# A fused Mamba-2 scan and PReLU MLP on one Trainium2 core: the state products of a pair moved to stand between the outputs' products of the pair in front and their copies

## The chip, the cores and the metric

The kernel runs on one core of one Trainium2 chip. The core has a matrix engine (TensorE, PE in the profile; its weight loads are listed as PEld), a vector engine (VectorE, DVE), a scalar engine (ScalarE, ACT), a general engine (GpSimd, POOL) and a queue that issues transfers (SyncE, SP). Each engine works through its own list of instructions in order and waits on semaphores for the others. The metric is the time of one execution on the device in microseconds. Three runs of the kernel before gave 380.07 in the median, from 380.0 to 380.35.

## The reference

The first half is a chunked state-space scan (Mamba-2's SSD form) over 4 batches, 8 heads, 768 steps, head dimension 32 and state dimension 16; the second half is an MLP with PReLU over the resulting 3072 tokens of width 256, with d_ff = 2048. Cut to what is computed:

```python
# scan, per batch and head, chunk by chunk
L  = exp(cum_i - cum_j) * causal            # decays between steps of a chunk
M  = (C @ B.T) * L                          # Gram products times decays
y  = M @ x  +  (C @ state) * exp(cum)       # within the chunk + from the state before it
state = exp(sum(log a)) * state + sum_j decay_from_j * B_j (x) x_j
# MLP
h = y @ w_in                                # 256 -> 2048
g = max(h, 0) + alpha * min(h, 0)
out = g @ w_out                             # 2048 -> 256
```

All of it is in fp32.

## The kernel before

**The scan.** The kernel uses chunks of Q = 128 steps, 24 of them over the four batches (six per batch), and treats two at a time: pair 0 to pair 11 (`pair(gp)`, L416). A pair is a Python generator; every `yield` ends a stage, and `ssm(gp, stages)` (L905) lets it run on by that many stages. What a pair issues:

- the transposes of B and C (PE, L469) and their copy out of PSUM (ACT, L472, tile bc);
- the decays inside a chunk, by scans on DVE (L438, tile dec), eight per pair;
- C split over even and odd heads (ACT, L484, tile cz) and C times the decay from the chunk's start (POOL, L487, `c_decayed`, tile cd);
- B times the decay to the chunk's end (POOL, L385, `pair_loads`, tile bn);
- the **state products** bn x x (PE, L520, `added`), into a tile here called dps; the array is split in two by columns for them (128*64);
- the new states from them (DVE, L532; ACT, L529, for the first chunk of a batch) and their masked form sm (POOL, L535), both in `states`. The last pair of a batch (pairs 2, 5, 8, 11) needs one of its two blocks only;
- the Gram products C x B (PE, L570, `products_bc`), in four banks: two of the pool ps_s and, for pairs from 4 on, two of the pool ps_h (`spare()`), and their product with the decays (DVE, L606);
- the **outputs' products** (PE, L622 from the state and L629 within the chunks), into two tiles y, and their copies to SBUF (ACT, L636, tile xT).

**The MLP.** Four chunks make a group of 512 tokens (GC = 4, GT = 512); there are six groups. Group 0 is computed in the prologue by ordinary matmuls (`hidden`, `output`). Groups 1 to 5 take one level of a Strassen-like scheme with seven products in place of eight: `quad(g, z, after)` (L761) makes the four blocks of the hidden layer for a quarter z of d_ff (seven products `first`, L773, in two PSUM banks of ps_h, A and Y), applies PReLU (`prelu`, L751: ACT writes alpha times h, L756, and DVE takes the maximum, L758, column half by column half) to the blocks g12, g22, g21 and g11 in that order, and makes their differences on POOL (tc_, L807; ta, tb, td, L816). Its blocks go through seven products with w_out (`product`, L747) during the following quad. So the main loop (L1022) has 20 quads; z runs from 0 to 3 in each group.

**The order.** The schedule is written out by hand. `quad` calls `after(1)` to `after(14)` between its own steps, and `after(j)` issues what the tables hold for the place (z, j): `with_gram`/`without` the products of the quad before, `late_sums` the sums of weights for the scheme (POOL, L715; in the first three quads of the loop), `steps` one more stage of a pair, and the other places `combine` and `finish` (the end of the group before), `token_sums` (POOL, L727) and `pair_loads`. In group g the pairs 2g + 2 and 2g + 3 are worked on, for group g + 1 of the MLP. In the list below "(0, 9)" is the place z = 0, j = 9; a pair's two halves repeat with z + 2.

For pairs from 4 on (`fine`), the stages before the change stand at: transposes at (1, 12); the scans at (1, 14), (2, 1), (2, 2), (2, 5), with cz at the last; L520, L532, L535 and L487 at (2, 9); L570 and half of L606 at (2, 13); the rest of L606 at (3, 1); L622, L629 and L636 at (3, 5). bn is made at (1, 3) and (3, 8). The place j = 5 lies between DVE's L792 and the product of `first` that goes to the block c22 (DVE, L796); j = 9 between the PReLU of g21 and the product for g11; L802 is ACT's copy of m1 back to the bank Y, which that product adds to.

**Banks.** ps_s and ps_h have two banks each. Tiles from `ss_tile` take the banks of ps_s in turn: one for the transposes, one for dps, two for the Gram products, two for y, six per pair.

**Loads.** SP's list holds each pair's loads (`load_pair`, L139: ap, nat = B and C, xt = x, and abc, the decays spread over partitions); from pair 5 on they are issued at the start of the quads z = 0 and z = 2, more than a quad in front of the pair's transposes.

Of the kernel before, what the change touches and what calls it, by code (L numbers as in the profile page):

```python
# [9 lines left out]
F32 = mybir.dt.float32  # L10
U32 = mybir.dt.uint32
U16 = mybir.dt.uint16
ALU = mybir.AluOpType
# [9 lines left out]
def kernel(  # L23
# [25 lines left out]
    nc = tc.nc  # L49
# [6 lines left out]
    P = 128  # L56
    Q = 128
# [51 lines left out]
    def ss_tile():  # L109
        if early[0] is None:  # L110
            return ps_s.tile([P, 512], F32, name="ss")
        early[0] += 1
        i = early[0] % (3 if ident_p else 4)
        return ps_s.tile([P, 512], F32, name="ss") if i < 2 else bank(i)
# [211 lines left out]
    held = {}  # L326
    bns = {}

    def identity_bank():


        m5_bank.append(bank(3))
        nc.scalar.copy(out=m5_bank[0][:, HT:], in_=ident_h[:, :HT])
        ident_p.append(m5_bank[0][:, HT:])
# [42 lines left out]
    def pair_loads(gp):  # L377

        b, c = divmod(2 * gp, CPB)
        nat, abc, xt, ap = loads["p", gp]  # L380

        bn = work.tile([P, 2, H * N], F32, name="bn")
        i, bi = divmod(b, 2)
        pj = prt[i].rearrange("p (b h c) -> p b c h", b=2, h=H)[:, bi, c : c + 2]
        nc.gpsimd.tensor_tensor(  # L385
            out=bn.rearrange("p k (h n) -> p k h n", h=H),
            in0=nat[:, 0].rearrange("p k (h n) -> p k h n", h=H),
            in1=pj.unsqueeze(3).to_broadcast([P, 2, H, N]), op=ALU.mult)
        return bn
# [22 lines left out]
    def spare():  # L412

        return ps_h.tile([P, GT], F32, name="hp", tag="hp")

    def pair(gp):  # L416

        b, c = divmod(2 * gp, CPB)
        nat, abc, xt, ap = loads["p", gp]
        last = c + 2 == CPB  # L420
        dec = work.tile([P, 2, H, Q], F32, name="dec")
        dv = dec.rearrange("p k h t -> p k (h t)")

# [37 lines left out]
            yield  # L461


        tp = spare() if gp == 1 else ss_tile()
        if gp == 0:
            keep_warm(tp, 3, Q)
# [19 lines left out]
        def c_decayed():  # L486
            nc.gpsimd.tensor_tensor(out=cd.rearrange("p k t -> p (k t)"), in0=ct, in1=pf,  # L487
                                    op=ALU.mult)

        fine = gp >= 2 * GC // 2  # L490
        if gp < 2:
            spread_c()
        if gp == 0:
# [2 lines left out]
            dps = spare()  # L496
            keep_warm(dps, 6, Q)
            yield
        bn = bns.pop(gp) if gp in bns else pair_loads(gp)
        if gp == 1:  # L500
            c_decayed()
            dps = spare()
# [1 line left out]
        elif gp:  # L504
            yield

        nk = 1 if last else 2  # L510
        st = [masked.get(b)]
        new = work.tile([P, 2, P], F32, name="state")
        sm = work.tile([P, 2, P], F32, name="sm")

        def added(dps):
            dps = dps.rearrange("p (k m) -> p k m", m=P)
            for k in range(nk):
                for w in range(KC):
                    ws = slice(64 * w, 64 * w + 64)
                    nc.tensor.matmul(dps[ws, k], bn[:, k, ws], xt[:, k, w * P : (w + 1) * P],  # L520
                                     start=True, stop=True, tile_position=(0, 64 * w),
                                     skip_group_check=True)
            return dps

        def states(dps):
            for k in range(nk):
                old = state.get(b)
                if old is None:
                    nc.scalar.copy(out=new[:, k], in_=dps[:, k])  # L529
                else:  # L530
                    e = (k + 1) * Q - 1
                    nc.vector.scalar_tensor_tensor(out=new[:, k], in0=old, scalar=pf[:, e : e + 1],  # L532
                                                   in1=dps[:, k], op0=ALU.mult, op1=ALU.add)
                state[b] = new[:, k]
            nc.gpsimd.tensor_tensor(out=sm[:, :nk], in0=new[:, :nk],  # L535
                                    in1=hmask.unsqueeze(1).to_broadcast([P, nk, P]), op=ALU.mult)
            st.extend(sm[:, k] for k in range(nk))
            masked[b] = st[-1]

        if fine:  # L540
            for k in range(2):
                for w in range(2):
                    half_decays(k, w)
                    if k == 1 and w == 1:
                        spread_c()
                    yield
        else:
            if gp > 1:
                states(added(ss_tile()))
                c_decayed()  # L550
            decays(0)
            if gp == 1:
                dps = added(dps)
            if gp:
                yield
            if gp != 1:
                decays(1)
            if gp > 1:
                spread_c()
# [24 lines left out]
        if gp == 0:  # L584
            gram = products_bc()
            dps = added(dps)
            yield
            c_decayed()
            times(dec[:, :, :2], one_less(gram))
        elif gp == 1:  # L590
            gram = products_bc()
            g0 = one_less(gram)
            yield
            decays(1)
            states(dps)
            times(dec[:, :, :2], g0)
        else:
            if fine:
                states(added(ss_tile()))
                c_decayed()  # L600
            yield
            gram = products_bc()
        for i, r in enumerate(r for r in ((2, 3, 0, 1) if fine else (3, 2, 1, 0) if gp > 1 else range(4))
                              if r in gram):
# [6 lines left out]
        yield  # L611


        y = [ss_tile()[:, : 2 * Q].rearrange("p (k t) -> p k t", k=2) for w in range(KC)]
        if gp < 2:
            keep_warm(y[0].rearrange("p k t -> p (k t)"), 2 - gp)
        begun = False
# [7 lines left out]
        for k in range(2):  # L625
            for w in range(KC):
                for q in range(4):
                    h = 4 * w + q
                    nc.tensor.matmul(y[w][32 * q : 32 * q + 32, k], xt[:, k, h * D : (h + 1) * D],  # L629
                                     dec[:, k, h], start=False, stop=True,  # L630
                                     tile_position=(0, 32 * q), skip_group_check=True)
        g, q = divmod(2 * gp, GC)
        if q == 0:
            xts[g] = xtp.tile([P, KC, GT], F32, name="xT")
# [344 lines left out]
    for f in range(FIRST, NF):  # L979
        if f in (5, 10):  # L980
            load_pair(3 + f // 10)
        if f == 5:
            load_rows(1)
        hidden(0, f)
        if f <= 10:
            ssm(2)
        if f >= 9:
            ssm(3)
        for i in {FIRST: (5,), FIRST + 1: (6, 7)}.get(f, ()):
            convert_a(*pieces[i])  # L990
        convert_next(first=f > FIRST)
        if f == 8:
            bns[3] = pair_loads(3)
        if f == 8:
            rows_clamp(1)
            held["pr"] = rows_scan(1)
            rows_out(1)
        output(f - FIRST)
        if f in in_steps:
            weight_sums(wi, in_sums, 0, in_steps[f])  # L1000
    early[0] = None
    token_sums(1)
    ssm(2 * GC // 2, 2)


    steps = {(0, 1): 0, (0, 2): 0, (0, 5): 0, (0, 9): 0, (0, 13): 0, (1, 1): 0, (1, 5): 0,
             (1, 12): 1, (1, 14): 1, (2, 1): 1, (2, 2): 1, (2, 5): 1, (2, 9): 1, (2, 13): 1,
             (3, 1): 1, (3, 5): 1, (3, 12): 2, (3, 14): 2}

    late_sums = {(0, 2): ((wqt, out_sums, 0, 0),), (0, 4): ((wqt, out_sums, 0, 1),),  # L1010
# [11 lines left out]
    for i in range(NZ * (NG - 1)):  # L1022
        g, z = divmod(NZ + i, NZ)
        nxt = 2 * g + 2

        def after(j, g=g, z=z, i=i, nxt=nxt):
            places = with_gram if nxt < NP and z % 2 == 0 else without
            if i and j in places:
                product(*divmod(NZ + i - 1, NZ), places[j])
            if i == 0:  # L1030
                for f, half in last_out.get(j, ()):
                    output(NF - LATE + f, half)
            if (i, j) in ((0, 13), (1, 2)):
                store_first(i)
            for args in late_sums.get((i, j), ()):
                weight_sums(*args)
            if g > 1 and z == 0 and j in (5, 9, 13, 14):
                if j == 5:
                    comb[0] = combine(g - 1)
                next(comb[0], None)  # L1040
            if g > 1 and z in (1, 3) and j == 11:
                finish(g - 1, z // 2)
            if nxt + steps.get((z, j), NP) < NP:
                ssm(nxt + steps[z, j])
            if nxt < NP and (z, j) == (3, 7):
                token_sums(g + 1)
            ahead = nxt + {(1, 3): 1, (3, 8): 2}.get((z, j), NP)
            if ahead < NP:
                if ahead == 6:
                    rows_turn(1, held["pr"])  # L1050
                bns[ahead] = pair_loads(ahead)

        comb = [None] if i == 0 else comb
        if z == 0 and nxt < NP:
            load_pair(nxt + 1)
        if z == 2 and nxt + 2 < NP:
            load_pair(nxt + 2)
        quad(g, z, after)
# [31 lines left out]
```

## Time and profile before

| | |
|---|---|
| median of three runs | 380.07 us (380.0 to 380.35) |
| the profiled execution | 380.35 us, of it 378.6 span |
| PE busy | 368.0 us, 97% of the span |
| PEld busy | 294.0 us, 78% |
| DVE busy | 248.1 us, 66% |
| POOL busy | 201.3 us, 53% |
| ACT busy | 182.0 us, 48% |
| TensorE clock granted | 1.000 |
| L520, L629 one matmul instruction | 273 ns, x80 and x384 |
| L532 (DVE) | 340 ns, x16 |
| L535 (POOL), 128x256 | 0.73 us |
| L487 (POOL) | 0.73 us, x12 |
| L385 (POOL) | 0.64 us, x12 |

The profile is one execution on the chip. A line of the time line gives the start (us from the span's start), the time from first start to last end, the engine, the line of the program, the operation, the tiles written and read with their shapes, and the number of instructions merged in it; at its end stand the engine's idle time in front of it and what ended it. PE's matmuls overlap in the pipeline, so the distance from one start to the next tells more than a duration. An fp32 product of 128 rows and 256 columns appears as two matmul instructions.

### The profile page before, as it was taken

To read this page: it belongs to the slowest core of one execution; us is meant where nothing else is said; L and a number is where in the kernel's file an instruction comes from. 1 tells how busy PE (TensorE), PEld (TensorE's weight loads), DVE (VectorE), ACT (ScalarE), POOL (GpSimd) and SP (SyncE) were. 2 spreads that over 40 slices of the span, in tenths; PEclk is the share of its full clock that TensorE was granted. 3 is DMA by queue.
4 is the path that set the end of the run, shared out by engine and by line. 5 is a ranking of instruction groups with operands and counts; after the bars stand their busy time and mean duration, and the time that the engine had idled before them with its cause. 6 is when DMAs were issued, how large, how long until landed. Compare 5 with 4: busy or idle time off the path is not lost.

```text
span 378.6 us, 6134 instructions
## 1 busy us (share of the span) xinstructions
PE 368.0 (97%) x2223; PEld 294.0 (78%) x2223; DVE 248.1 (66%) x462; ACT 182.0 (48%) x384; POOL 201.3 (53%) x211
## 2 busy tenths in 40 slices
PE   8989999999999999999999999999999999999996
PEld 7666665677788788788788788788788788888884
DVE  7996979976448548738638748638747735554364
ACT  2647856435355245444445445435525525543541
POOL 4875666677919644724645535455354345355412
PEclk9999999999999999999999999999999999999999
DMA  7979998911176201004603702801801000101003
GB/s 136 196 156 331 253 281 187 179 29 56 59 123 116 65 3 55 2 0 69 140 3 55 153 2 47 164 0 35 173 4 22 9 0 11 19 0 30 1 0 83
DMA packets 121878, 30.71 MB, mean 81 GB/s; under 512 B 93736, under 2 KB 117752, under 8 KB 121848
## 3 DMA queue, kind: packets, MB, share of 16 engines
q1 hardware_dynamic: 116736, 29.74, 35.8%
q10 hardware_dynamic: 5112, 0.59, 1.1%
q8 instruction: 17, 0.28, 0.3%
q14 instruction: 13, 0.11, 0.1%
HBM read 26.98 MB, written 3.34 MB: 80 GB/s over the span
## 4 chain that ended last, share of the span: by engine, by line
PE 70%; DVE 15%; ACT 7%; DMA 3%; issue 2%; POOL 2%; SPq 0%; POOLq 0%; DVEq 0%; ACTq 0%
PE hp L773 28%; PE bank L747 26%; ACT gt L756 5%; DVE gt L758 5%; DVE dec L438 3%; PE bank L686 3%; PE ss L629 2%; PE hp L648 2%; PE hp L570 2%; DMA rows<-in_a_dram 2%; PE ss L622 1%; DVE wr L239 1%; DVE gt L652 1%; PE hp L663 1%; DVE state L532 1%
## 5 line engine op out<-in xcount | busy, mean ns | idle before, releaser
L758 DVE SCALAR_TENSOR_TENSOR gt<-hp,s_mul,gt 128x256 f32<-128x256 f32 x120 | 58.0, 483 | 51.3 <-ACT gt L756 50.2
L816 POOL TENSOR_TENSOR gt<-gt 128x512 f32<-128x512 f32 x58 | 73.8, 1272 | 33.0 <-PE bank L747 19.2
L756 ACT ACTIVATE gt<-hp,s_alpha 128x256 f32<-128x256 f32 x120 | 56.6, 474 | 66.8 <-DVE gt L758 36.4
L747 PE MATMUL bank<-gt,w_out 128*128 128x256 f32 x320 | 82.6, 382 | 0.0
L807 POOL TENSOR_TENSOR gt<-gt 128x512 f32<-128x512 f32 x20 | 25.4, 1272 | 81.1 <-DVE gt L758 70.7
L747 PEld LDWEIGHTS bank<-gt,w_out 128*128 128x128 f32 x320 | 60.1, 190 | 10.6 <-issue 2.3
L747 PE MATMUL bank<-gt,ws 128*128 128x256 f32 x240 | 58.3, 379 | 0.0
L747 PEld LDWEIGHTS bank<-gt,ws 128*128 128x128 f32 x240 | 45.1, 190 | 5.8
L438 DVE TENSOR_TENSOR_SCAN dec<-abc,bank 128x256 f32<-128x256 f32 x80 | 48.1, 661 | 0.0
L773 PE MATMUL hp<-xs,w_in 128*128 128x256 f32 x160 | 42.8, 390 | 0.0
L773 PE MATMUL hp<-xT,w_in 128*128 128x256 f32 x160 | 41.9, 384 | 0.0
L773 PE MATMUL hp<-xs,ws 128*128 128x256 f32 x160 | 41.1, 379 | 0.0
L792 DVE TENSOR_TENSOR hp<-hp,u 128x512 f32<-128x512 f32 x20 | 14.0, 700 | 37.5 <-ACT u L790 37.1
L773 PEld LDWEIGHTS hp<-xs,w_in 128*128 128x128 f32 x160 | 28.7, 189 | 7.7 <-issue 1.9
L773 PEld LDWEIGHTS hp<-xT,w_in 128*128 128x128 f32 x160 | 29.7, 190 | 5.2 <-ACT hp L802 1.0
L773 PEld LDWEIGHTS hp<-xs,ws 128*128 128x128 f32 x160 | 30.4, 190 | 4.1
L781 ACT COPY m<-hp 128x512 f32<-128x512 f32 x20 | 11.7, 586 | 41.0 <-PE hp L773 41.0
L686 PE MATMUL bank<-w_out,gt 128*128 128x256 f32 x128 | 31.0, 384 | 0.0
L686 PEld LDWEIGHTS bank<-w_out,gt 128*128 128x128 f32 x128 | 23.7, 190 | 6.6 <-issue 3.7
L796 DVE TENSOR_TENSOR c<-hp,m 128x512 f32<-128x512 f32 x20 | 13.6, 682 | 19.2 <-PE hp L773 19.2
L648 PE MATMUL hp<-xT,w_in 128*128 128x512 f32 x48 | 22.8, 598 | 0.5 <-DVE gt L652 0.3
L790 ACT COPY u<-hp 128x512 f32<-128x512 f32 x20 | 11.7, 586 | 22.5 <-PE hp L773 22.5
(156 smaller groups left out, 556.0 us busy)
## 6 DMA issues: line engine op xcount, KB each, us to landing
abc<-z SPq DMA_DIRECT2D x20, 512.0 KB, 5.3
raw<-in_moe_w_in_dram SPq DMA_DIRECT2D x8, 512.0 KB, 5.4
raw<-in_moe_w_out_dram SPq DMA_DIRECT2D x8, 512.0 KB, 6.5
xt<-in_x_dram SPq DMA_DIRECT2D x24, 128.0 KB, 2.9
out_dram<-o_sb SPq DMA_DIRECT2D x32, 64.0 KB, 1.9
nat<-in_B_dram SPq DMA_DIRECT2D x22, 64.0 KB, 3.4
nat<-in_C_dram SPq DMA_DIRECT2D x22, 64.0 KB, 2.8
ap<-pf SPq DMA_DIRECT2D x11, 128.0 KB
```

The lines of the kernel that those rows point to most:

```text
L438: nc.vector.tensor_tensor_scan(out=dv[:, k, hs], data0=abc[k][:, hs], data1=ident_p[0], initial=0.0, op0=ALU.mult, op1=ALU.add)
L648: nc.tensor.matmul(hp, w_in[:, k, f * P : (f + 1) * P], xts[g][:, k], start=(k == 0), stop=(k == KC - 1))
L686: nc.tensor.matmul(pos[0][t // 2][:, t % 2], gt[:, t * Q : (t + 1) * Q], w_out[:, f], start=(f == 0 and t % 2 == 0), stop=(f == NF - 1), s ...
L747: nc.tensor.matmul(ms[g][i][:, h], w, blocks[g, z][n][:, p], start=(q == 0 and h == 0), stop=(q == NQ - 1), skip_group_check=True)
L756: nc.scalar.mul(o[:, p], h[:, p], s_alpha[:, fs[p]])
L758: nc.vector.scalar_tensor_tensor(out=o[:, p], in0=h[:, p], scalar=s_mul[:, fs[p]], in1=o[:, p], op0=ALU.mult, op1=ALU.max)
L773: nc.tensor.matmul(to[:, p], w(2 * z + p), b, start=start and p == 0, stop=True, skip_group_check=True)
L781: nc.scalar.copy(out=m1, in_=A)
L792: nc.vector.tensor_tensor(out=Y, in0=Y, in1=u2, op=ALU.add)
L796: nc.vector.tensor_tensor(out=c22, in0=A, in1=m5, op=ALU.add)
L807: nc.gpsimd.tensor_tensor(out=tc_, in0=g22, in1=g12, op=ALU.subtract)
L816: eng.tensor_tensor(out=o, in0=x0, in1=x1, op=ALU.subtract)
```

## The change

The function `prelu` is left as it is. What the diff does:

- `added` and `states` (L520, L529, L532, L535) become the first two stages of a pair from 4 on, in front of its transposes; the block from the transposes to `c_decayed` is moved behind them unchanged.
- dps no longer takes a bank of its own: it lies in the second half of the bank of the second y of the pair in front (`beside`). Only pair 4, whose predecessor is not `fine`, takes a bank from `ss_tile`.
- A new `yield` stands between L629 and L636. At (1, 5) and (3, 5) four stages follow each other: the outputs' products of a pair, the state products of the next one, the copies L636 of the first, the states of the next.
- The steps at (0, 9) and (2, 9) go. `c_decayed` moves to the stage at (0, 5) and (2, 5), behind cz.
- `pair_loads` moves from (1, 3) and (3, 8) to (0, 9) and (2, 9); for pair 6 it takes `rows_turn` (L365: a transpose on PE, L368, and a copy on ACT, L372) with it. For pair 4 it is issued at f = 14 of the prologue, and that pair's first four stages run in front of the loop instead of its first two.

```diff
@@ -326,6 +326,8 @@
     held = {}
     bns = {}
+    beside = {}
+
     def identity_bank():
@@ -418,6 +420,7 @@
         b, c = divmod(2 * gp, CPB)
         nat, abc, xt, ap = loads["p", gp]
         last = c + 2 == CPB
+        fine = gp >= 2 * GC // 2
         dec = work.tile([P, 2, H, Q], F32, name="dec")
         dv = dec.rearrange("p k h t -> p k (h t)")
@@ -461,51 +464,6 @@
             yield
-        tp = spare() if gp == 1 else ss_tile()
-        if gp == 0:
-            keep_warm(tp, 3, Q)
-        for i in range(2):
-            for k in range(2):
-                nc.tensor.transpose(tp[:, (2 * i + k) * P : (2 * i + k + 1) * P], nat[:, i, k],
-                                    ident)
-        bc = work.tile([P, 4, Q], F32, name="bc")
-        nc.scalar.copy(out=bc.rearrange("p i t -> p (i t)"), in_=tp)
-        bh, ct = bc[:, :2], bc[:, 2:].rearrange("p k t -> p (k t)")
-        cz = czp.tile([P, 2, 2, Q], F32, name="cz")
-        cd = work.tile([P, 2, Q], F32, name="cd")
-
-        def spread_c():
-            for e in range(2):
-                o = cz[:, e].rearrange("p k t -> p (k t)")
-                if gp == 0 and e == 1:
-                    nc.gpsimd.tensor_scalar(out=o, in0=ct, scalar1=par[:, e : e + 1],
-                                            scalar2=None, op0=ALU.mult)
-                else:
-                    nc.scalar.mul(o, ct, par[:, e : e + 1])
-
-        def c_decayed():
-            nc.gpsimd.tensor_tensor(out=cd.rearrange("p k t -> p (k t)"), in0=ct, in1=pf,
-                                    op=ALU.mult)
-
-        fine = gp >= 2 * GC // 2
-        if gp < 2:
-            spread_c()
-        if gp == 0:
-            rows_turn(0, held.pop("pr"))
-            bns[0] = pair_loads(0)
-            dps = spare()
-            keep_warm(dps, 6, Q)
-            yield
-        bn = bns.pop(gp) if gp in bns else pair_loads(gp)
-        if gp == 1:
-            c_decayed()
-            dps = spare()
-            ahead[1] = spread(z, 1, lambda w: ss_tile())
-        elif gp:
-            yield
-
-
-
         nk = 1 if last else 2
         st = [masked.get(b)]
@@ -513,7 +471,7 @@
         sm = work.tile([P, 2, P], F32, name="sm")
         def added(dps):
-            dps = dps.rearrange("p (k m) -> p k m", m=P)
+            dps = dps[:, : 2 * Q].rearrange("p (k m) -> p k m", m=P)
             for k in range(nk):
                 for w in range(KC):
                     ws = slice(64 * w, 64 * w + 64)
@@ -538,11 +496,63 @@
             masked[b] = st[-1]
         if fine:
+            bn = bns.pop(gp) if gp in bns else pair_loads(gp)
+            dps = added(beside.pop(gp) if gp in beside else ss_tile()[:, : 2 * Q])
+            yield
+            states(dps)
+            yield
+
+
+        tp = spare() if gp == 1 else ss_tile()
...
+        if not fine:
+            bn = bns.pop(gp) if gp in bns else pair_loads(gp)
+        if gp == 1:
+            c_decayed()
+            dps = spare()
+            ahead[1] = spread(z, 1, lambda w: ss_tile())
+        elif gp:
+            yield
+
+        if fine:
             for k in range(2):
                 for w in range(2):
                     half_decays(k, w)
                     if k == 1 and w == 1:
                         spread_c()
+                        c_decayed()
                     yield
         else:
             if gp > 1:
@@ -595,10 +605,8 @@
             states(dps)
             times(dec[:, :, :2], g0)
         else:
-            if fine:
-                states(added(ss_tile()))
-                c_decayed()
-            yield
+            if not fine:
+                yield
             gram = products_bc()
         for i, r in enumerate(r for r in ((2, 3, 0, 1) if fine else (3, 2, 1, 0) if gp > 1 else range(4))
                               if r in gram):
@@ -611,7 +619,10 @@
         yield
-        y = [ss_tile()[:, : 2 * Q].rearrange("p (k t) -> p k t", k=2) for w in range(KC)]
+        ys = [ss_tile() for w in range(KC)]
+        y = [t[:, : 2 * Q].rearrange("p (k t) -> p k t", k=2) for t in ys]
+        if fine:
+            beside[gp + 1] = ys[1][:, 2 * Q :]
         if gp < 2:
             keep_warm(y[0].rearrange("p k t -> p (k t)"), 2 - gp)
         begun = False
@@ -629,6 +640,8 @@
                     nc.tensor.matmul(y[w][32 * q : 32 * q + 32, k], xt[:, k, h * D : (h + 1) * D],
                                      dec[:, k, h], start=False, stop=True,
                                      tile_position=(0, 32 * q), skip_group_check=True)
+        if fine:
+            yield
         g, q = divmod(2 * gp, GC)
         if q == 0:
             xts[g] = xtp.tile([P, KC, GT], F32, name="xT")
@@ -989,6 +1002,8 @@
         for i in {FIRST: (5,), FIRST + 1: (6, 7)}.get(f, ()):
             convert_a(*pieces[i])
         convert_next(first=f > FIRST)
+        if f == 14:
+            bns[4] = pair_loads(4)
         if f == 8:
             bns[3] = pair_loads(3)
         if f == 8:
@@ -1000,11 +1015,11 @@
             weight_sums(wi, in_sums, 0, in_steps[f])
     early[0] = None
     token_sums(1)
-    ssm(2 * GC // 2, 2)
-
-
-    steps = {(0, 1): 0, (0, 2): 0, (0, 5): 0, (0, 9): 0, (0, 13): 0, (1, 1): 0, (1, 5): 0,
-             (1, 12): 1, (1, 14): 1, (2, 1): 1, (2, 2): 1, (2, 5): 1, (2, 9): 1, (2, 13): 1,
+    ssm(2 * GC // 2, 4)
+
+
+    steps = {(0, 1): 0, (0, 2): 0, (0, 5): 0, (0, 13): 0, (1, 1): 0, (1, 5): 0,
+             (1, 12): 1, (1, 14): 1, (2, 1): 1, (2, 2): 1, (2, 5): 1, (2, 13): 1,
              (3, 1): 1, (3, 5): 1, (3, 12): 2, (3, 14): 2}
     late_sums = {(0, 2): ((wqt, out_sums, 0, 0),), (0, 4): ((wqt, out_sums, 0, 1),),
@@ -1042,9 +1057,14 @@
                 finish(g - 1, z // 2)
             if nxt + steps.get((z, j), NP) < NP:
                 ssm(nxt + steps[z, j])
+
+                if j == 5 and z % 2:
+                    for p in (1, 0, 1):
+                        if nxt + z // 2 + p < NP:
+                            ssm(nxt + z // 2 + p)
             if nxt < NP and (z, j) == (3, 7):
                 token_sums(g + 1)
-            ahead = nxt + {(1, 3): 1, (3, 8): 2}.get((z, j), NP)
+            ahead = nxt + {(0, 9): 1, (2, 9): 2}.get((z, j), NP)
             if ahead < NP:
                 if ahead == 6:
                     rows_turn(1, held["pr"])
```

More of the change, by code (lines that the diff above doesn't have):

```diff
@@ L461, in pair, with added, states @@
             yield
+        nk = 1 if last else 2
+        st = [masked.get(b)]
+        new = work.tile([P, 2, P], F32, name="state")
+        sm = work.tile([P, 2, P], F32, name="sm")
+        def added(dps):
+            dps = dps[:, : 2 * Q].rearrange("p (k m) -> p k m", m=P)
+            for k in range(nk):
+                for w in range(KC):
+                    ws = slice(64 * w, 64 * w + 64)
+                    nc.tensor.matmul(dps[ws, k], bn[:, k, ws], xt[:, k, w * P : (w + 1) * P],
+                                     start=True, stop=True, tile_position=(0, 64 * w),
+                                     skip_group_check=True)
+            return dps
+        def states(dps):
+            for k in range(nk):
+                old = state.get(b)
+                if old is None:
+                    nc.scalar.copy(out=new[:, k], in_=dps[:, k])
+                else:
+                    e = (k + 1) * Q - 1
+                    nc.vector.scalar_tensor_tensor(out=new[:, k], in0=old, scalar=pf[:, e : e + 1],
+                                                   in1=dps[:, k], op0=ALU.mult, op1=ALU.add)
+                state[b] = new[:, k]
+            nc.gpsimd.tensor_tensor(out=sm[:, :nk], in0=new[:, :nk],
+                                    in1=hmask.unsqueeze(1).to_broadcast([P, nk, P]), op=ALU.mult)
+            st.extend(sm[:, k] for k in range(nk))
+            masked[b] = st[-1]
+        if fine:
[4 more added lines that the diff above has]
+            yield
         tp = spare() if gp == 1 else ss_tile()
@@ L505, in pair @@
             yield
[L510 to L515, printed above, removed]
-            dps = dps.rearrange("p (k m) -> p k m", m=P)
[L517 to L529, printed above, removed]
-                else:
[L531 to L538, printed above, removed]
         if fine:
```

## The prediction

> **What bounds the kernel now.** I read the page's chain first, then the time line of the main loop, where the change sits, then the waits of the lines that it touches.
>
> ```profile
> PE 70%; DVE 15%; ACT 7%; DMA 3%; issue 2%; POOL 2%; SPq 0%; POOLq 0%; DVEq 0%; ACTq 0%
> ```
>
> PE carries the chain for most of the span, DVE and ACT for 22%. The time line says where. In the odd quads of a group (z = 1 and 3), which hold the outputs' products of a pair (L622, L629), PE issues without a gap:
>
> ```profile
> 163.06 1.08 PE L629 MATMUL ss<-dec,xt 128*32 128x128 f32 x32
> 163.99 0.65 ACT L636 COPY xT<-ss 128x256 f32<-128x256 f32 x2 [1.52 <-PE ss L629]
> 164.07 1.13 PE L773 MATMUL hp<-xs,w_in 128*128 128x256 f32 x4
> 165.03 1.03 PE L773 MATMUL hp<-xT,ws 128*128 128x256 f32 x4
> 165.24 0.69 DVE L796 TENSOR_TENSOR c<-hp,m 128x512 f32<-128x512 f32 x1 [2.04 <-PE hp L773]
> ```
>
> The reader is to see that ACT (1.52 us idle) and DVE (2.04) have room here and PE none: what is added to PE is paid. In the even quads (z = 0 and 2), which hold the state products L520 and the Gram products L570, it is otherwise (pair 7):
>
> ```profile
> 180.95 0.58 ACT L802 COPY hp<-m 128x512 f32<-128x512 f32 x1
> 181.19 0.66 PE L520 MATMUL ss<-xt,bn 128*64 128x128 f32 x8
> ...
> 181.77 1.13 PE L773 MATMUL hp<-xT,w_in 128*128 128x256 f32 x4
> ...
> 182.48 0.99 ACT L756 ACTIVATE gt<-hp,s_alpha 128x256 f32<-128x256 f32 x2 [0.55 <-DVE gt L758]
> ...
> 183.39 0.72 DVE L532 SCALAR_TENSOR_TENSOR state<-state,ap,ss 128x128 f32<-128x128 f32 x2
> ...
> 184.03 0.48 DVE L758 SCALAR_TENSOR_TENSOR gt<-hp,s_mul,gt 128x256 f32<-128x256 f32 x1
> ...
> 185.05 0.48 DVE L758 SCALAR_TENSOR_TENSOR gt<-hp,s_mul,gt 128x256 f32<-128x256 f32 x1 [0.54 <-ACT gt L756]
> 185.59 0.48 PE L570 MATMUL hp<-cz,bc 32*128 32x256 f32 x1 [0.32 <-DVE gt L758]
> ```
>
> The Gram products need both hp banks, so their second half starts only when the PReLU of g11 has left the second one. In all eight quads it starts 1.56 us after g11's first L758 (184.03 to 185.59 here; 94.52 to 96.08, 125.02 to 126.58, 154.64 to 156.20, 213.39 to 214.95, 242.62 to 244.18, 272.13 to 273.69, 301.37 to 302.93): ACT and DVE taking turns on one bank are the gate. PE, whose first half takes 0.65, is there 0.0 to 0.9 us earlier. So L520 here is mostly cover-filling: without it PE would wait for L802 (ends 181.53, next product 181.77) and again at the gate.
>
> **The change, part by part.** prelu itself is not edited. What moves is, for pairs 4 to 11, L520, L532 and L535 out of the even quad into the odd quad before it (pair 4's in front of the loop), the products c·decay (POOL L487) from (z even, 9) to (z even, 5), bn (POOL L385) to (z even, 9), and prt's transpose and copy (L368, L372) from (3, 8) to (2, 9).
>
> *New place on PE (cost).* From L520's first issue to the next product is 0.59 us for two blocks (x8: 181.19 to 181.77, 151.96 to 152.55) and 0.37 for one (x4: 122.21 to 122.58, the last pair of a batch). With the slower first issue on each side (0.86 became 0.96) the detour is 0.79 and 0.57. In the new place L629 already pays for leaving and re-entering the full array, so I take 0.59 and 0.37. Bounds: 0.43 and 0.22 if nothing but the streams counts (eight of 0.108, two at a time), 0.79 and 0.57 if the whole detour is paid again. Four pairs of two blocks (6, 7, 9, 10) and three of one (5, 8, 11): 4 x 0.59 + 3 x 0.37 = 3.5 us (2.4 to 4.9). Pair 4's products come at 81.73, between back-to-back L686 and L469: 0.75. Together 4.2 us (3.1 to 5.7).
>
> *Old place (gain).* Only the gate counts. What ends last for g11's first L758 once L532 and L529 are gone: pair 4, L715 on DVE, which moves up with it, 0.64 earlier; pair 5, g21's L758, 0.24 earlier, less most of prt's copy (0.22), now in ACT's queue there: 0.1; pair 6, ACT's mul behind L835, 0.18; pair 7, g21's L758, 0.53; pair 8, ACT's mul behind L835, 0.02; pair 9, 0.25 (L529 goes from ACT too); pair 10, 0.41; pair 11, 0.26. Sum 2.4 us. PE arrives earlier by L802's slack and the saved exit, 0.1 to 0.3, which just keeps it in front of the gate.
>
> *POOL.* Its queue is in order, and one row shows what happens when DVE wants SBUF operands while POOL works:
>
> ```profile
> 121.47 1.28 POOL L715 TENSOR_TENSOR w_out<-w_out 128x512 f32<-128x512 f32 x1
> ...
> 121.66 1.36 DVE L758 SCALAR_TENSOR_TENSOR gt<-c,s_mul,gt 128x256 f32<-128x256 f32 x1
> ```
>
> The instruction takes 0.47 elsewhere; here it ended 0.27 after POOL's. The c·decay product (0.73) now stands between the L715s of the first and third quad and pushes the last one into this L758. The third quad loses 0.3 to 0.7 at the gate (0.4 taken; it gains 0.4 if both L758 slip between two L715s); in the first the 0.4 that DVE waits for ACT covers it. In later quads c·decay, bn and prt's work meet idle POOL time (5.10 in front of L807 at pair 7), at no cost. If nat came late, bn would hold L816 behind it; for pair 8 nat's last part is issued at 178.37 and lands about 3.4 later, bn is due near 183.
>
> The Trainium skill, "Trainium Architecture — The Big Picture", section "What this means for kernel authors", says that VectorE and GpSimd share one port pair under an exclusive lock. The row agrees with it. By that rule also the L727s, which sm (L535) now pushes towards g22 in z = 3, would each cost a wait; DVE's 0.40 idle before g21 covers it.
>
> *New waits in the odd quad.* dps shares a bank with y[1]. ACT and DVE wait for each other on the two halves of one bank already (36.4 us of L756 waiting for L758), so I expect the second copy L636 to wait for L520 and L532 for that copy. Queued behind: on ACT the mul of g12 (1.51 us of room), on DVE c22, L796 (2.04 of room; L532 ends about 1.7 after L629, c22's operand comes at 1.8), on POOL sm and then, in z = 3, four L727 whose result is first read a quad later. Nothing on the path. SP's queue keeps its order: loads are not moved.
>
> *Sum.* 4.2 - 2.4 + 0.4 - 0.1 (L368's gap in z = 3) = +2.1 us. The profiled execution took 380.35 (span 378.6 and 1.75 around it), 0.3 over the median of 380.07; on the median that is 382.2. Ends: 3.1 - 2.8 = +0.3 and 5.7 - 1.4 = +4.3.
>
> The skill speaks for the change: "TensorEngine Tiling (Array Packing)", "Key Properties", says that changing the tiling mode drains the array. Put next to L629, L520 costs one mode change fewer per pair, and by that rule alone the sum would be about -1.6 us (an estimate: eight times the 0.2 by which 0.79 exceeds 0.59). The trace agrees on the price (0.10 in front, 0.16 and 0.10 behind L520), but the place left is one where PE waits anyway.
>
> **Rivals.**
> *A: as summed,* 382.2, from 381.0 to 383.5.
> *B: nearly free.* L520 overlaps L629's tail (both split the columns) and the third quad's L758 slip through: +0.3 to +0.6, 380.5. For it: eight matmuls stream only 0.43. Against: L570 to L520, from split array to split array, still shows a gap at 11.40.
> *C: faster.* The even quads give back the whole detour, because the gate follows PE rather than the turns of ACT and DVE: 5 x 0.79 + 3 x 0.57 = 5.7 against 3.1 to 4.2 paid, -1.5 to -2.6, about 378. It decides from 0.53 us of gate per quad on (4.2 over 8); the chain view gives 0.30. Against: g11's first product is done at about 182.3, before ACT is free for it at 182.95, in pair 7. For it: pairs 8, 9 and 11 have PE within 0.2 of the gate, so both limits are close and another order of events could move them together.
> *D: slower still.* The one-bank order makes c22 late in the odd quads, or POOL's queue holds L816: from 0.1 us after c22's due time on it reaches the PReLU chain. At 0.2 to 0.4 in seven quads, 383.6 to 385.
>
> **How the numbers follow.** Chances: A 0.55, B 0.13, C 0.17, D 0.15. About 0.2% (0.76 us) can be told from no change here. Faster is C and a trace of B, 0.18; same is the rest of B and A's lowest end, 0.14; slower A and D, 0.68. The range 380.2 to 384.0 leaves out C and D's upper part, some 2 in 10.
>
> **What would show it.** Right: L520 directly behind L629, the next L773 about 1.6 us after L629's first issue instead of 1.0; in even quads L773 waiting for ACT L802 and L570 for DVE L758, with odd quads 0.4 to 0.6 longer and even ones 0.0 to 0.6 shorter. L758 (from c) at 0.9 or more in the third quad. Wrong: even quads shorter by 0.6 or more throughout (C), L520 taking under 0.45 beside L629 (B), L796 waiting for L532 (D).

## The result, and the profile after

The changed kernel took 382.24 us (median of four runs, 381.66 to 383.0) against 380.03 (379.58 to 380.35): ratio 1.006, 95% interval 1.0037 to 1.0083. It is slower, by 2.2 us; the profiled execution took 381.83, its span 379.9 against 378.6. The mechanism of the forecast held: the state products are paid in full in the odd quads, and the even quads give back less.

The chain of the page, after:

```profile
PE 79%; DVE 8%; ACT 7%; SPq 2%; DMA 2%; issue 1%; ACTq 0%; POOL 0%; POOLq 0%
```

PE's share is 79% where it was 70%, and DVE's 8% where it was 15%, but most of this is not the change. In the stretch ahead of the first quad the chain held 29 us of PE and 27 of DVE before, and 57 and 4 after; the page of `e8_decay_late` below, which is the changed kernel but for one POOL instruction per pair, shows 70% and 12% again. From the first quad on, PE's part went from 234 to 241 us and DVE's from 31 to 25. The waits say more. PE's, after, from the list of who waited for whom (us in total, times, longest):

```profile
PE hp L786 <- ACT hp L815: 2.6, 8, 0.4
...
PE hp L580 <- DVE gt L771: 1.1, 2, 0.6
```

and before:

```profile
PE hp L570 <- DVE gt L758: 2.2, 5, 0.9
```

Eight times PE now waits for ACT's copy of m1 to Y (L802 before, L815 after) where it used to run the state products, a wait that the list of before does not have. The wait at the gate, the start of the second half of the Gram products (L570 before, L580 after), has fallen from 2.2 us in five places to 1.1 in two.

The odd quad that was shown of before, in the time line after (L640 is the former L629, L478 the former L520, L649 L636, L490 L532, L786 L773, L809 L796):

```profile
163.42 1.08 PE L640 MATMUL ss<-dec,xt 128*32 128x128 f32 x32
164.35 0.37 ACT L649 COPY xT<-ss 128x256 f32<-128x256 f32 x1 [1.52 <-PE ss L640]
164.43 0.66 PE L478 MATMUL ss<-xt,bn 128*64 128x128 f32 x8
165.02 1.13 PE L786 MATMUL hp<-xs,w_in 128*128 128x256 f32 x4
165.13 0.37 ACT L649 COPY xT<-ss 128x256 f32<-128x256 f32 x1 [0.41 <-PE ss L478]
165.54 0.73 DVE L490 SCALAR_TENSOR_TENSOR state<-state,ap,ss 128x128 f32<-128x128 f32 x2 [1.98 <-ACT xT L649]
165.98 1.03 PE L786 MATMUL hp<-xT,ws 128*128 128x256 f32 x4
166.19 0.69 DVE L809 TENSOR_TENSOR c<-hp,m 128x512 f32<-128x512 f32 x1
```

From L640's first issue to the next product of the MLP it is 1.60 us (163.42 to 165.02), before 1.01 (163.06 to 164.07): the state products cost 0.59 beside the outputs' products. The second copy waits for them and the state updates wait for that copy, but L809 starts 1.17 us after the first issue of the product that it reads (165.02 to 166.19), as before (164.07 to 165.24): those waits are off the path.

The even quad of pair 7, after (L771 is the former L758, L769 L756, L580 L570); the first line is the quad's first product:

```profile
173.33 1.03 PE L786 MATMUL hp<-xT,w_in 128*128 128x256 f32 x4
...
181.18 1.03 PE L786 MATMUL hp<-xs,w_in 128*128 128x256 f32 x4
...
182.54 1.13 PE L786 MATMUL hp<-xT,w_in 128*128 128x256 f32 x4 [0.33 <-ACT hp L815]
...
183.43 0.84 ACT L769 ACTIVATE gt<-hp,s_alpha 128x256 f32<-128x256 f32 x2 [0.55 <-DVE gt L771]
...
183.94 0.88 DVE L771 SCALAR_TENSOR_TENSOR gt<-hp,s_mul,gt 128x256 f32<-128x256 f32 x2 [0.54 <-ACT gt L769]
...
185.36 0.48 DVE L771 SCALAR_TENSOR_TENSOR gt<-hp,s_mul,gt 128x256 f32<-128x256 f32 x1 [0.54 <-ACT gt L769]
...
185.90 0.48 PE L580 MATMUL ss<-cz,bc 32*128 32x256 f32 x2
```

Two lines of the same quad before, beside those of the prediction:

```profile
172.38 1.03 PE L773 MATMUL hp<-xT,w_in 128*128 128x256 f32 x4
...
180.23 1.03 PE L773 MATMUL hp<-xs,w_in 128*128 128x256 f32 x4
```

The place of the state products is empty and PE idles there: from one product's first issue to the next it is 1.36 us (181.18 to 182.54), before with the state products between them 1.54 (180.23 to 181.77). The gate did move: the quad starts at 173.33, so the second half of the Gram products starts 12.57 us into it (185.90); before 13.21 (185.59 less 172.38).

**Where the time went.** The next table gives each quad's length, from the first issue of its first product (`first` into A from b11) to that of the next quad, read from the time lines of PE.

| quad (pair whose state products were in it, or now are) | before | after | difference | forecast |
|---|---|---|---|---|
| 1st, z = 0 (4 left) | 16.80 | 16.15 | -0.65 | -0.64 |
| 2nd (5 added) | 14.37 | 14.75 | +0.38 | +0.37 |
| 3rd, z = 2 (5 left) | 15.26 | 15.36 | +0.10 | +0.3 |
| 4th (6 added) | 14.49 | 14.97 | +0.48 | +0.5 |
| 5th (6 left) | 15.13 | 14.96 | -0.17 | -0.18 |
| 6th (7 added) | 14.16 | 14.74 | +0.58 | +0.59 |
| 7th (7 left) | 15.23 | 14.59 | -0.64 | -0.53 |
| 8th (8 added) | 14.38 | 14.75 | +0.37 | +0.37 |
| 9th (8 left) | 14.98 | 14.96 | -0.02 | -0.02 |
| 10th (9 added) | 14.38 | 14.96 | +0.58 | +0.59 |
| 11th (9 left) | 14.85 | 14.59 | -0.26 | -0.25 |
| 12th (10 added) | 14.15 | 14.75 | +0.60 | +0.59 |
| 13th (10 left) | 15.37 | 14.96 | -0.41 | -0.41 |
| 14th (11 added) | 14.38 | 14.75 | +0.37 | +0.37 |
| 15th (11 left) | 14.85 | 14.59 | -0.26 | -0.26 |
| 16th to 19th | 50.50 | 50.50 | 0.0 | 0 |

The odd quads gained 3.36 us, the even ones lost 2.31; the loop is 1.05 longer. In front of it stand pair 4's state products: from the last L686 of the prologue to the first quad it was 2.16 us (80.01 to 82.17) and is 2.90 (79.50 to 82.40), +0.74. Together +1.79; the rest of the difference of the medians (2.2) lies within what the prologue varies by (at the end).

### The profile page after: what moved, and what is told of

It is laid out like the page before. It is cut to its first block, busy times and chain, and to the rows that moved or that the text cites. A ratio compares the mean times of both kernels' runs of the same rounds, so it can differ in the third digit from the quotient of the medians.

```text
span 379.9 us, 6122 instructions
## 1 busy us (share of the span) xinstructions
PE 369.1 (97%) x2223; PEld 295.2 (78%) x2223; DVE 250.0 (66%) x462; ACT 182.2 (48%) x384; POOL 201.0 (53%) x211
## 4 chain that ended last, share of the span: by engine, by line
PE 79%; DVE 8%; ACT 7%; SPq 2%; DMA 2%; issue 1%; ACTq 0%; POOL 0%; POOLq 0%
PE hp L786 28%; PE bank L760 26%; PE bank L699 7%; PE hp L661 6%; ACT gt L769 5%; DVE gt L771 4%; PE ss L640 2%; PE hp L580 2%; PE ss L633 1%; PE ss L478 1%; DMA nat<-in_B_dram 1%; PE ss L511 1%; PE hp L676 1%; DVE dec L441 1%; SPq L163 1%
## 5 line engine op out<-in xcount | busy, mean ns | idle before, releaser
L771 DVE SCALAR_TENSOR_TENSOR gt<-hp,s_mul,gt 128x256 f32<-128x256 f32 x120 | 57.7, 483 | 50.7 <-ACT gt L769 49.5
L769 ACT ACTIVATE gt<-hp,s_alpha 128x256 f32<-128x256 f32 x120 | 56.3, 472 | 65.2 <-DVE gt L771 34.7
L786 PE MATMUL hp<-xT,w_in 128*128 128x256 f32 x160 | 41.9, 384 | 2.6 <-ACT hp L815 2.6
L786 PE MATMUL hp<-xs,w_in 128*128 128x256 f32 x160 | 42.8, 390 | 0.0
L786 PE MATMUL hp<-xs,ws 128*128 128x256 f32 x160 | 41.1, 379 | 0.0
L786 PEld LDWEIGHTS hp<-xT,w_in 128*128 128x128 f32 x160 | 29.7, 190 | 9.4 <-ACT hp L815 5.8
L786 PEld LDWEIGHTS hp<-xs,w_in 128*128 128x128 f32 x160 | 28.8, 189 | 7.5 <-ACT u L803 1.3
L786 PEld LDWEIGHTS hp<-xs,ws 128*128 128x128 f32 x160 | 30.4, 190 | 4.1
L493 POOL TENSOR_TENSOR sm<-state,bmask 128x256 f32<-128x256 f32 (+1 forms) x12 | 7.9, 661 | 34.3 <-DVE state L490 34.1
L803 ACT COPY u<-hp 128x512 f32<-128x512 f32 x20 | 11.7, 585 | 22.5 <-PE hp L786 22.5
```

Source lines behind the costliest of these rows:

```text
L769: nc.scalar.mul(o[:, p], h[:, p], s_alpha[:, fs[p]])
L771: nc.vector.scalar_tensor_tensor(out=o[:, p], in0=h[:, p], scalar=s_mul[:, fs[p]], in1=o[:, p], op0=ALU.mult, op1=ALU.max)
L786: nc.tensor.matmul(to[:, p], w(2 * z + p), b, start=start and p == 0, stop=True, skip_group_check=True)
L803: nc.scalar.copy(out=u2, in_=A)
```

## The experiments

Each run is compared with runs of the kernel before taken beside it, whose median was 379.62 us for the first four and 379.51 for the last three.

**The price of the new place.** `e3_twice` is the kernel before with the products issued a second time:

```diff
-        y = [ss_tile()[:, : 2 * Q].rearrange("p (k t) -> p k t", k=2) for w in range(KC)]
+        ys = [ss_tile() for w in range(KC)]
+        y = [t[:, : 2 * Q].rearrange("p (k t) -> p k t", k=2) for t in ys]
...
+        if fine:
+            added(ys[1][:, 2 * Q :])
         g, q = divmod(2 * gp, GC)
```

> The kernel before with the state products of pairs 4 to 11 issued a second time, between the outputs' products and their copies, into the second half of the second bank of y; nobody reads them. It is the price of the new place by itself, nothing is taken from the old one. Theory: five pairs of two blocks at 0.59 us and three of one at 0.37, all on PE in the odd quads: +4.1 us, 384.1. Rival B (the products overlap the tail of the outputs' products): five at 0.43 and three at 0.22, +2.8 us, 382.8. If odd quads had room on PE: 380.0.

Measured 383.52 against 379.62: ratio 1.0101, 1.0086 to 1.0116, +3.9 us. Odd quads +0.60, +0.37, +0.58, +0.58, +0.37, +0.59, +0.58, +0.37 (pairs 4 to 11), +4.04 in all; every even quad within 0.03 of before. Time line, the odd quad with pair 6's outputs:

```profile
163.03 1.08 PE L630 MATMUL ss<-dec,xt 128*32 128x128 f32 x32
164.04 0.66 PE L520 MATMUL ss<-xt,bn 128*64 128x128 f32 x8
164.63 1.13 PE L776 MATMUL hp<-xs,w_in 128*128 128x256 f32 x4
```

The products start when the outputs' products have run their 1.01 us and take 0.59 themselves. Rival B, an overlap with the tail, falls, and so does any room on PE in odd quads.

**What the old place cost.** `e2_no_products` leaves the state products of pairs 4 to 11 out:

```diff
             if fine:
-                states(added(ss_tile()))
+                ss_tile()
+                states(bmask.rearrange("p (k m) -> p k m", m=P))
                 c_decayed()
```

> The kernel before without the state products of pairs 4 to 11 (left out: the states take a constant tile in SBUF in their place, so the outputs that follow from the states are others); everything else stays in its place. Theory (gate): PE only waits longer in the even quads, for ACT's copy of m1 and for the gate, which DVE sets; 0.0 to 0.3 us gained in all, 379.7 to 380.0. Rival C: the whole detour comes back, 5.7 us, 374.3.

Measured 379.78 against 379.62: ratio 1.0001, 0.9991 to 1.0011. No quad differs by more than 0.03 us. Time line, pair 7 (L759 is L758 before, L803 L802):

```profile
180.15 0.58 ACT L803 COPY hp<-m 128x512 f32<-128x512 f32 x1
...
180.79 1.13 PE L774 MATMUL hp<-xT,w_in 128*128 128x256 f32 x4 [0.33 <-ACT hp L803]
...
182.59 0.73 DVE L532 SCALAR_TENSOR_TENSOR state<-state,ap,bmask 128x128 f32<-128x128 f32 x2
...
183.24 0.48 DVE L759 SCALAR_TENSOR_TENSOR gt<-hp,s_mul,gt 128x256 f32<-128x256 f32 x1
...
184.79 0.48 PE L570 MATMUL hp<-cz,bc 32*128 32x256 f32 x1 [0.51 <-DVE gt L759]
```

PE's wait at the gate has only grown, from 0.32 to 0.51 us, and a new one of 0.33 stands in front of g11's product. In the even quads the products were free, as the forecast had it: they filled time in which PE would have waited. Rival C (5.7 us back) falls.

**Only the products moved.** `e7_products_only` is the changed kernel with the state updates, their masking and C times decay back in the even quads:

```diff
             dps = added(beside.pop(gp) if gp in beside else ss_tile()[:, : 2 * Q])
             yield
-            states(dps)
-            yield
...
-            if not fine:
-                yield
+            if fine:
+                states(dps)
+                c_decayed()
+            yield
             gram = products_bc()
```

> The changed kernel, but only the state products (and bn) in the new place; state updates, masking and C times decay stay in the even quads where they were before. Theory: the full cost of the new place, 3.5 us, and 0.75 for pair 4 in front of the loop, and no gain, since the state updates still stand in front of the gate: +4.2 us, 384.2; odd quads as in the changed kernel, even quads as before. Rival C (the even quads follow PE): they give back 5.7 us, 378.6.

Measured 383.59 against 379.62: ratio 1.0112, 1.0092 to 1.0132, +4.0 us. Odd quads as in the changed kernel (+0.38, +0.48, +0.58, +0.36, +0.59, +0.59, +0.37), even ones as before (within 0.03). Pair 7:

```profile
184.37 0.72 DVE L490 SCALAR_TENSOR_TENSOR state<-state,ap,ss 128x128 f32<-128x128 f32 x2
...
185.00 0.48 DVE L770 SCALAR_TENSOR_TENSOR gt<-hp,s_mul,gt 128x256 f32<-128x256 f32 x1
...
186.56 0.48 PE L577 MATMUL hp<-cz,bc 32*128 32x256 f32 x1 [0.51 <-DVE gt L770]
```

So the two halves of the change separate: moving the products alone costs all of it and gives nothing, and the changed kernel gets nothing back without moving the state updates on DVE.

**Only the state updates moved.** `e1_gaps` is the kernel before, the products in their old place, with the updates in the gaps of the PReLU:

```diff
+            if p == 0 and between is not None:
+                between()
...
         first(A, lambda q: wi[:, q, 1, 1], t4)
-        prelu(g21, A, z, 1)
+        after("A")
+        prelu(g21, A, z, 1, between=lambda: after("B"))
...
         first(Y, lambda q: wi[:, q, 0, 1], b21)
-        prelu(g11, Y, z, 0)
+        prelu(g11, Y, z, 0, between=lambda: after("C"))
```

The place "A" issues the state products, "B" the first update, "C" the second with the masking and C times decay; they take the place of j = 9 in the table of steps.

> The kernel before, with the state products left in the even quads and only the two state updates on DVE (ACT for the first chunk of a batch) put elsewhere: one between the two halves of the PReLU of g21, one between those of g11, where DVE waits 0.54 us for ACT. Theory (gate): the turns of ACT and DVE, with the state updates among them, set when the second half of the Gram products starts; the even quads get shorter by the smaller of what the gate moves and what PE waits there: 0.64, 0.24, 0.18, 0.38, 0.02, 0.0, 0.41 and 0.19 us for pairs 4 to 11, together 2.1, odd quads unchanged: 378.0 us, ratio 0.9946. Rival C (the even quads follow PE and the detour of the state products): nothing changes, 380.0. The kernel would then be better than both.

Measured 377.35 against 379.62: ratio 0.994, 0.9925 to 0.9955. Even quads -0.65, -0.29, -0.17, -0.51, -0.02, -0.13, -0.41, -0.27, together -2.45 where 2.1 was expected; odd quads unchanged. Pairs 7, 9 and 11 gave 0.13, 0.13 and 0.08 more than expected: I had capped them by a first half of the Gram products of 0.65 us, but where nothing holds the second half it follows sooner (0.54 after the first in pair 7, 183.20 to 183.74). Pair 7 (L770 is L758, L768 L756, L531 L532, L576 L570):

```profile
180.60 0.48 DVE L770 SCALAR_TENSOR_TENSOR gt<-hp,s_mul,gt 128x256 f32<-128x256 f32 x1 [0.40 <-ACT gt L768]
181.00 0.34 DVE L531 SCALAR_TENSOR_TENSOR state<-state,ap,ss 128x128 f32<-128x128 f32 x1
181.12 0.99 ACT L768 ACTIVATE gt<-hp,s_alpha 128x256 f32<-128x256 f32 x2 [0.55 <-DVE gt L770]
...
181.63 1.00 DVE L770 SCALAR_TENSOR_TENSOR gt<-hp,s_mul,gt 128x256 f32<-128x256 f32 x2 [0.28 <-ACT gt L768]
...
182.55 0.34 DVE L531 SCALAR_TENSOR_TENSOR state<-state,ap,ss 128x128 f32<-128x128 f32 x1
```

An update of 0.34 fits into the 0.54 in which DVE waits for ACT: the wait behind it shrinks to 0.28 and nothing else moves. This settles the gate, and the kernel is faster than both. The even quads give back as much as in the changed kernel (2.45 against 2.31), without its price in the odd ones. Quad by quad there are two differences: the third lacks the changed kernel's collision on POOL (below), and pairs 7 and 9 gain 0.13 less each. There the products' leaving helps once the updates are gone: in the changed kernel, `e2_no_products` and `e7_products_only` the Gram products of these two pairs start 12.0 us into the quad, before and here 12.18.

**POOL's moves alone.** `e4_pool_only`:

```diff
                     if k == 1 and w == 1:
                         spread_c()
+                        c_decayed()
...
                 states(added(ss_tile()))
-                c_decayed()
...
-            ahead = nxt + {(1, 3): 1, (3, 8): 2}.get((z, j), NP)
+            ahead = nxt + {(0, 9): 1, (2, 9): 2}.get((z, j), NP)
```

(and bn of pair 4 at f = 14).

> The kernel before with only the moves of C times decay to the place j = 5 of the even quads and of bn (with prt's transpose and copy for pair 6) to j = 9; state products and state updates stay. Theory: POOL is idle where the pieces land, except in the third quad, where the sums of weights stand and the last one is pushed by 0.73 us into the L758 that reads c22: that quad 0.0 to 0.4 us longer, every other the same, 380.0 to 380.4 from 380.0. Rival D (POOL's queue holds L816 or bn waits for its load): 0.1 to 0.3 in most even quads, 381 to 382.

Measured 379.83 against 379.51: ratio 1.0004, 0.9993 to 1.0016, which is no difference that can be told. The quads tell more: the third is 0.32 longer, the fourth 0.11 shorter (prt's transpose has left it), all others within 0.02. Time line of the third:

```profile
120.55 2.09 DVE L758 SCALAR_TENSOR_TENSOR gt<-c,s_mul,gt 128x256 f32<-128x256 f32 x2
120.90 1.45 POOL L715 TENSOR_TENSOR w_out<-w_out 128x512 f32<-128x512 f32 x1
```

The pair of L758 took 1.76 before, and POOL's sum, too, got longer (1.28). Rival D's part of it, POOL holding other even quads up, falls.

**C times decay back.** `e8_decay_late` is the changed kernel with `c_decayed` in its old place, a stage of its own at (0, 9) and (2, 9).

> The changed kernel with C times decay alone back at j = 9 of the even quads. Theory: in the third quad the last sum of weights starts 0.7 us earlier again and the two L758 that read c22 take 1.8 us together, as before, in place of 2.02; that quad is 0.2 us shorter (15.36 to about 15.15), all others the same: 382.0 from 382.2. If the third quad stays at 15.36, its loss comes from prt's copy alone.

Measured 381.47 against 379.51: ratio 1.0045, 1.003 to 1.0061. The third quad went from 15.36 to 15.01, further than the 15.15 expected; all others as in the changed kernel but the first, 16.22 after 16.15. The two L771 that read c22 took 1.66 in place of 2.02:

```profile
121.88 1.66 DVE L771 SCALAR_TENSOR_TENSOR gt<-c,s_mul,gt 128x256 f32<-128x256 f32 x2
```

The collision on POOL is nearly the whole of the third quad's loss: without it the quad is 0.25 shorter than before, and in `e1_gaps`, which does not move prt's copy, 0.29; that leaves about 0.04 for the copy.

**The collision taken away.** `e5_gaps_sum` is `e1_gaps` with one sum of weights later:

```diff
-                 (2, 6): ((wqt, out_sums, 4, 2),), (2, 8): ((wqt, out_sums, 4, 3),)}
+                 (2, 6): ((wqt, out_sums, 4, 2),), (2, 10): ((wqt, out_sums, 4, 3),)}
```

> The kernel with the state updates in the gaps of the PReLU (e1_gaps), and the last sum of weights of the third quad on POOL issued at j = 10, behind L807, in place of j = 8. Theory (one SBUF port pair): the L758 that reads c22 no longer meets POOL there and takes 0.5 in place of 1.3 us; DVE is 0.4 earlier at g21, the gate moves by that, and PE, which waits 0.21 there, by 0.2: the third quad 14.97 to about 14.75, everything else as in e1_gaps, 377.2. If the 1.3 us had another cause, nothing changes.

Measured 376.54 against 379.51: ratio 0.992, 0.9905 to 0.9934, the fastest version here. The third quad went from 14.97 to 14.60; 0.2 was expected. Every other quad as in `e1_gaps`. Its time line:

```profile
119.56 0.88 DVE L770 SCALAR_TENSOR_TENSOR gt<-c,s_mul,gt 128x256 f32<-128x256 f32 x2
...
121.82 1.26 POOL L727 TENSOR_TENSOR w_out<-w_out 128x512 f32<-128x512 f32 x1
```

Without POOL's sum beside them the two L758 (L770 here) took 0.88 in place of the 1.73 of `e1_gaps`. That the 0.9 us belong to POOL's overlapping work is shown by these three runs; that the resource is a port is the word of the Trainium skill ("Trainium Architecture — The Big Picture", "What this means for kernel authors"), and no run here shows more than the collision.

## Why the prediction was right, point by point

- *What bounds the kernel.* The 22% of the chain that lie on DVE and ACT were put down to the even quads. The odd and even quads are rightly told apart by the time line, but nearly half of DVE's part before (27 of 58 us) lies ahead of the first quad, so the page's shares say less of the loop than the prediction took from them.
- *The sum.* 382.2 forecast, 382.24 measured. So close a hit owes something to chance: on the profiled execution the sum said +2.1, the quads and pair 4 make +1.79, and the medians differ by 2.2.
- *New place on PE.* 0.59 and 0.37, 0.75 for pair 4: measured 0.58 to 0.60, 0.37 to 0.38, and 0.74. Pair 6's quad shows +0.48 because prt's transpose has left it, which alone makes it 0.11 shorter (`e4_pool_only`). Both bounds were wide of it. The lower one, 0.43, stands for matmuls that stream without a break, and `e3_twice` shows that a break is paid between the outputs' products in four column strips and the state products in two: 0.20 us from the last start of the ones to the first of the others (163.84 to 164.04), as much as before to the next product on the full array (163.86 to 164.07).
- *Old place.* The claim that only the gate counts was the load-bearing one, and `e2_no_products` and `e1_gaps` show it from both sides. Six of the eight sizes agree within 0.02. Pair 5's is told under POOL; pair 7's was 0.64 for 0.53. There PE delivers g11's first product earlier when the state products are gone, and ACT's two muls take 0.84 in place of 0.99; they take 0.84 in `e2_no_products` and `e7_products_only` too, and 0.99 in `e1_gaps`, which keeps the products there. I had written that this product was done at about 182.3, well in front of ACT; the last of its matmuls ends at 182.90, and the second mul starts only at 183.00.
- *POOL.* The collision in the third quad came as told, 0.35 us by `e8_decay_late` against 0.4 taken. Counted with pair 5's own term, the quad came out at +0.10 for +0.3: the term for prt's copy took too much off the gain, since without the collision the quad is 0.25 shorter, not 0.1. That the first quad's collision would be covered was not put to the test, since there was hardly a collision to cover: POOL's last sum there ran from 89.72 to 90.99, and the two L771 that read c22 started at 90.80 and took the 0.88 that they take alone.
- *New waits.* The second copy waits for the state products (0.41), the updates for the copy (1.98 of idle time in front of them), as forecast; c22 was not late.
- *Rivals.* B fell to `e3_twice`, C to `e2_no_products` and `e7_products_only`, D to `e4_pool_only` and to c22's place in the time line after. The rule of the Trainium skill that the prediction names for the change ("TensorEngine Tiling (Array Packing)", "Key Properties"), that a change of the tiling mode drains the array, goes with a real saving of 0.2 us per pair: the detour is 0.79 in the old place and 0.59 in the new one. But the old place was one where PE would have waited, so the 0.79 was free and the 0.59 is not.

## What to carry to other kernels

A price on the busiest engine counts only where that engine is the limit: PE was busy for 97% of the span, and yet the state products cost nothing in the even quads and their full time in the odd ones. Before moving work, ask of each stretch what ends last in it, and separate the instructions of a step by engine: here the products on PE stood well, and only their consumers on DVE stood in the way. Where two engines take turns on one bank, each has a gap in every turn; here an instruction of 0.34 us put into a gap of 0.54 was free.

## What the runs showed of the hardware beyond that

- Where DVE's L758 with two operands in SBUF met two of POOL's sums in a row, not only DVE took longer: POOL's second sum did as well, 1.45 in place of 1.27 to 1.28 (in `e4_pool_only` at 120.90 and in the changed kernel at 121.91).
- The prologue is not as steady as the loop. The first quad starts at 82.17, 81.93, 81.37, 81.22 and 80.72 us in the profiles of the kernel before, `e1_gaps`, `e2_no_products`, `e3_twice` and `e5_gaps_sum`, whose instructions up to there are the same, while quads repeat within 0.03. A difference of medians under 1 us is better read quad by quad.
